# The second shift of VectorE's exponents as a transfer that adds a constant in place

## The chip, the cores and the metric

The kernel runs on one core of one Trainium2 chip. The metric is the device time of one execution in microseconds, the median of several runs. Five queues of instructions run beside each other: TensorE (PE) with its weight loads (PEld), VectorE (DVE), ScalarE (ACT), GpSimd (POOL) and SyncE (SP), which only issues transfers here. Each takes its instructions in the order of the program and waits on semaphores where it needs another's result.

## The reference

One transformer block with conditioning: six rows of modulation from `silu(c) @ w_mod`, then a layer norm, attention with 32 heads of 16 columns over 2,048 tokens, and a layer norm with a two-layer network of 1,376 columns.

```python
mod = (silu(c) @ w_mod).reshape(1, 6, 1, 512)       # sa, ca, ga, sb, cb, gb
h = layernorm(x) * (1 + ca) + sa
q, k, v = split(h @ wqkv)                            # 32 heads of 16
p = softmax(q @ k.T * 16 ** -0.5)                    # 2048 x 2048 for each head
x = x + ga * ((p @ v) @ wo)
h = layernorm(x) * (1 + cb) + sb
x = x + gb * (gelu(h @ w1 + b1) @ w2 + b2)
```

The attention asks for 32 x 2,048 x 2,048 exponentials, and that is most of the work.

## The kernel before

**Quads.** The attention goes through 32 quads: a block of 512 queries (four blocks) and four heads that sit on four groups of 32 partitions (eight such groups of heads). The last two quads are cut in halves of 256 queries, so that their end can begin earlier. For every quad there are 16 tiles of 128 keys and four heads, 64 tiles of 128 x 512 scores. Four heads' matmuls run side by side on PE, since each uses 32 rows or 32 columns of it.

**Two ways to an exponential.** A tile's scores are made by PE in a bank of PSUM (line 819) and then go one of two ways.

- ScalarE takes two or three banks at once and writes the exponential into `PB` as bfloat16 (line 1254). One matmul per tile then multiplies it with the values (line 1028).
- VectorE makes an approximation. The scores were scaled when `q` was made, so that 1,024 is one power of two. VectorE adds a bias and writes the sum as a 16-bit integer into `TB` (line 1349); read as a 16-bit float, these bits are roughly 2 to the score: exact at whole powers, straight between them. To flatten the error the kernel uses three such approximations, with the scores shifted by thirds of a power of two: the integers of the first (j = 0), the same plus `MJ[1]` (j = 1), the same plus `MJ[2]` (j = 2). Each has a matmul of its own, with the values scaled to match (`VE`, and `VV` for j = 1 and 2). So a tile on VectorE costs an evacuation, two shifts on VectorE (line 1383, for two tiles at once) and three matmuls with the values in place of one. Only six of the sixteen key tiles (`DKT`) have scaled values and may go this way.

Two tiles on VectorE make a unit. A unit's integers lie in a slot of `TB`; there are `NT` = 19 slots. A shift goes into the old slot if the matmuls that read it are done, and into a free slot otherwise. Before the change the second shift adds `MJ[2] - MJ[1]` to the result of the first.

**The order is planned when the program is built.** A planner walks through time with a clock for each engine and the cost of each instruction written in the code. At each moment the engine that is furthest behind takes its next step: `step_pe`, `step_act`, `step_dve`, or the GpSimd step. So the program's order on each engine comes out of these costs, and a small change moves everything behind it. `D_LOAD` is how much work VectorE may have ahead of it when PE makes scores for it (`dve_load` adds it up), `T_NEED` and `T_NEXT` how many slots must be free. Entries for the value matmuls are queued by head with the time at which they are expected (`put_entries`); PE takes them in that order. When PE has nothing that fits, the planner lets it issue a filler, a matmul with zeros (`pe_idle`, lines 1092 and 1095), so that its clock isn't lowered.

**GpSimd.** It scales the values, multiplies gates into weights, and multiplies each quad's output with the reciprocal of its sum (line 1328), which SP brings to it through DRAM as `rb`. The planner keeps VectorE's shifts and GpSimd's arithmetic apart in time: `plock` and `dlock` hold back the one while the other runs, and a dependency puts a GpSimd instruction beside one of VectorE's that reads PSUM.

The modulation, the projections, the layer norms and the network of the previous block (`sums`, `alone`) are fitted between by position. The last block's network stands alone at the end, from some 735 us on.

Of the kernel before, what the change touches and what calls it, by code (L numbers as in the profile page):

```python
# [10 lines left out]
ACT = mybir.ActivationFunctionType  # L11
ALU = mybir.AluOpType
# [3 lines left out]
I16 = mybir.dt.int16  # L16
F16 = mybir.dt.float16
# [3 lines left out]
P = 128  # L21
# [14 lines left out]
NV = 3  # L36
# [4 lines left out]
NPA = 5  # L41
NPB = 5
NP = 3 * NPA + 2 * NPB
NT = 19
KEEP = 0.72
NQM = 5
BIG = 8.0
# [2 lines left out]
D_BANKS = (6, 5)  # L50
BG_BANKS = (2, 5, 6)
BG_STRICT = False
D_LOAD = 2300.0
D_ALONE = 1400.0
A_SLACK = 1350.0
OVER = 180.0
# [7 lines left out]
LOCK_WAIT = 100.0  # L64
TIE = 60.0
T_NEED = 1
T_NEXT = 2
T_OPEN = 0.0
ROOT = 1000.0
ROOT_L = 700.0  # L70
# [17 lines left out]
def adaln_block(ctx: ExitStack, tc: tile.TileContext, A_x, A_wqkv, A_wo, B_x, B_w1, B_b1, B_w2, B_b2,  # L88
# [262 lines left out]
    pbp = att.enter_context(tc.tile_pool(name="pbp", bufs=1))  # L351
    PB = pbp.tile([P, NP, 512], BF16, name="PB")
    TB = pbp.tile([P, NT, 2, 512], I16, name="TB")
    RB = [odp.tile([P, 512], FP32, name=f"rb{par}") for par in range(2)]
    for par in range(2):
        nc.gpsimd.memset(RB[par], 0.0)
# [490 lines left out]
    def dve_load(t):  # L847
        w = max(0.0, clk["DVE"] - t)
        for s in evacs:
            w += 0.0 if s.only else s.dur  # L850
        for s in shifts:
            w += 331.0 * (NV - 1 - s["j"])
        w += 600.0 * sum(1 for x in d_fill)
        return w

# [53 lines left out]
    def pe_burst(t, z):  # L909
        bs = list(ZONES[z]) if z is not None else []  # L910
        x = EXTRA[z] if z is not None else None
        if x is not None and free[x] <= t and not (busy_sum[0] is None and reserve(t)):
            bs.append(x)
        take = []
        for r in lag_rows():
            if len(take) == len(bs):
                break
            if rowq[r] and item_ok(*rowq[r][0], t):
                take.append((r, 0))
        if z is not None and len(take) < len(bs):  # L920
            more = [(r, 1) for r, _ in take if len(rowq[r]) > 1 and item_ok(*rowq[r][1], t)]
            take += more[:len(bs) - len(take)]
        if z is not None and not take:
            return False
        picked = [(r, rowq[r][k]) for r, k in take]
        for r, x in picked:
            rowq[r].remove(x)
        used = [r for r, _ in take]
        dp = []
        if d_wanted(t):  # L930
            for r in d_rows(used):
                k = next_d(r, t)
# [12 lines left out]
                if u is None or len(u["it"]) + len(dp) == 2:  # L945
                    break
        if z is None and not dp:
            return False
        go("q")
        t0 = clk["PE"]  # L950
        rows = [r for r, _ in picked] + [r for _, r, _ in dp]
        first = len(set(rows))
        clk["PE"] = t0 + group(first) + (group(len(rows) - first) if len(rows) > first else 0.0)
        ready = clk["PE"] + L_PE
        qk([(b_, qi, kt, r) for (r, (qi, kt)), b_ in zip(picked, bs)] + [(b_, qi, kt, r) for b_, r, (qi, kt) in dp])
        for (r, (qi, kt)), b_ in zip(picked, bs):
            free[b_] = INF
        if z is not None:
            zone_busy[z] = True
            filled.append((z, [(qi, kt, r) for r, (qi, kt) in picked], clk["PE"] + L_PA))  # L960
        for b_, r, (qi, kt) in dp:
            free[b_] = INF
            if not units or len(units[-1]["it"]) == 2:
                s = next(i for i in range(NT) if tslot[i] <= t)
                tslot[s] = INF
                units.append({"it": [], "a": {"s": s}, "j": 0, "n": 0})
            u = units[-1]
            u["it"].append((qi, kt, r))
            todo[qi][r] += NV - 1
            claimed[qi][r] += 1  # L970
            d_fill.append((b_, u, len(u["it"]) - 1, ready))
            stat["d"] += 1
        stat["bursts"] += 1
        return True
# [363 lines left out]
    def step_dve(t):  # L1338
        if outs and outs[0][1] <= t:
            emit_out(outs.popleft()[0], t)  # L1340
            return True
        if d_fill and d_fill[0][3] <= t:
            b0, u, i, _ = d_fill[0]
            n = 1
            if (len(d_fill) > 1 and d_fill[1][1] is u and d_fill[1][3] <= t and d_fill[1][0] == b0 + 1):
                n = 2
            for _ in range(n):
                d_fill.popleft()
            made = nc.vector.tensor_scalar(out=TB[:, u["a"]["s"], i:i + n, :], in0=PS[:, b0:b0 + n, :], scalar1=T_BIAS,  # L1349
                                    scalar2=0.0, op0=ALU.add, op1=ALU.max)  # L1350
# [12 lines left out]
        if (units and units[-1]["n"] == 1 and len(units[-1]["it"]) == 1  # L1363
                and (sum(len(q) for q in rowq) < 10 or not any(left[units[-1]["it"][0][0]])
                     or t > units[-1]["at"] + 3000.0)):
            u = units[-1]
            u["it"].append(None)
            u["n"] = 2
            u["ok"] = t
            shifts.append(u)  # L1370
            put_entries(u, t)
        if take_evac("DVE", t):
            return True
        if run_alone("DVE", t):
            return True
        now = [] if plock[0] > t + LOCK_WAIT else [
            u for u in shifts if u["ok"] <= t and (u["a"].get("cons", INF) <= t or any(y <= t for y in tslot))]
        if now:
            u = max(now, key=lambda u: u["j"])
            a, j = u["a"], u["j"] + 1  # L1380
            n = sum(1 for it in u["it"] if it)
            s = a["s"] if a.get("cons", INF) <= t else next(i for i in range(NT) if tslot[i] <= t)
            made = nc.vector.tensor_scalar(out=TB[:, s, 0:n, :], in0=TB[:, a["s"], 0:n, :],  # L1383
                                           scalar1=float(MJ[j] - MJ[j - 1]), scalar2=None, op0=ALU.add)
            clk["DVE"] = max(t, plock[0] - 50.0) + 65.0 + 133.0 * n
            dve_log.append((clk["DVE"], made))
            dlock[0] = clk["DVE"]
            a["moved"] = clk["DVE"]
            if s != a["s"]:
                tslot[s] = INF  # L1390
                if "cons" in a:
                    tslot[a["s"]] = max(a["cons"], a["moved"])
            u["a"], u["j"], u["ok"] = {"s": s}, j, clk["DVE"] + 125.0
            if j == NV - 1:
                u["a"]["moved"] = 0.0
                shifts.remove(u)
                units.remove(u)
            put_entries(u, clk["DVE"] + L_DVE)
            return True
        return False  # L1400

    def put_entries(u, v):
        a, j = u["a"], u["j"]
        s = a["s"]
        cnt = [sum(1 for it in u["it"] if it)]

        def rel(done):
            cnt[0] -= 1
            if cnt[0] == 0:
                a["cons"] = done + L_FREE_D  # L1410
                if "moved" in a:
                    tslot[s] = max(a["cons"], a["moved"])

        for i, it in enumerate(u["it"]):
            if it is not None:
                qi, kt, r = it
                entries[qi][r].append((v, TB[:, s, i, :].bitcast(F16), kt, j, rel))

    def general_path():
        W_1, W_2, b1c = late["W_1"], late["W_2"], late["b1c"]  # L1420
# [88 lines left out]

    ENG = {"PE": step_pe, "ACT": step_act, "DVE": step_dve, "POOL": lambda t: run_alone("POOL", t)}
    rank = {"DVE": 0, "ACT": 1, "PE": 2, "POOL": 3}
    idle = dict.fromkeys(ENG, 0.0)
    tick = 20.0
# [55 lines left out]
```

## Time and profile before

| | |
|---|---|
| median of 3 runs | 764.57 us (764.04 to 765.09) |
| the profiled execution | 765.63 us |
| its span, first to last instruction | 763.9 us |
| mean granted TensorE clock | 0.992 |
| tiles through ScalarE | 377 pairs and 246 triples, 1,492 |
| tiles through VectorE | 556, and as many shifts of two |
| fillers on PE | 523 |
| GpSimd busy | 108.9 us of 763.9 |
| transfers issued by GpSimd | none |

A line of the groups names the program's line, the engine, the operation, what is written and read, their shapes and the count; behind the first bar stand the busy time of the group and the mean length of one instruction, behind the second the idle time of the engine just ahead of them and what ended it. An instruction's length includes its tail, in which the next one has begun already, so a mean times a count can exceed the busy time. A line of the stretches has the length, the busy time of PE, PEld, DVE, ACT and POOL with the number of instructions, the granted clock of PE, the share of time in which the transfer engines were busy, and GB/s.

### The profile page before, as it was taken

To read this page: it belongs to the slowest core of one execution; us is meant where nothing else is said; L and a number is where in the kernel's file an instruction comes from. 1 tells how busy PE (TensorE), PEld (TensorE's weight loads), DVE (VectorE), ACT (ScalarE), POOL (GpSimd) and SP (SyncE) were. 2 spreads that over 40 slices of the span, in tenths; PEclk is the share of its full clock that TensorE was granted. 3 is DMA by queue.
4 is the path that set the end of the run, shared out by engine and by line. 5 is a ranking of instruction groups with operands and counts; after the bars stand their busy time and mean duration, and the time that the engine had idled before them with its cause. 6 is when DMAs were issued, how large, how long until landed. Compare 5 with 4: busy or idle time off the path is not lost.

```text
span 763.9 us, 20459 instructions
## 1 busy us (share of the span) xinstructions
PE 737.2 (97%) x8478; PEld 258.7 (34%) x8478; DVE 700.5 (92%) x1450; ACT 721.7 (94%) x671; POOL 108.9 (14%) x134
## 2 busy tenths in 40 slices
PE   3999999999999999999999999999999999999997
PEld 2433233233333333332333333332333332333454
DVE  6859999699999999988999999999899999999982
ACT  2889999899999999999999999999999999999982
POOL 3460010214232010100001110100101110100110
PEclk9999999799999999999999999999999999999999
DMA  8300000041010000000010000000000000000000
GB/s 274 112 2 11 10 6 6 9 151 16 10 37 9 10 4 8 9 16 24 15 38 3 15 4 10 9 17 12 22 18 30 9 10 9 9 10 23 21 28 31
DMA packets 27572, 20.43 MB, mean 27 GB/s; under 512 B 13801, under 2 KB 23386, under 8 KB 27474
## 3 DMA queue, kind: packets, MB, share of 16 engines
q1 hardware_dynamic: 26946, 19.07, 9.0%
q8 instruction: 68, 1.11, 0.6%
q14 instruction: 30, 0.25, 0.1%
q10 hardware_dynamic: 528, 0.00, 0.0%
HBM read 16.45 MB, written 2.61 MB: 25 GB/s over the span
## 4 chain that ended last, share of the span: by engine, by line
PE 57%; ACT 26%; DVE 9%; issue 5%; DMA 2%; SPq 1%; POOL 0%; ACTq 0%; DVEq 0%
ACT PB L1254 23%; PE PS L819 20%; PE PS L1028 18%; PE PS L406 12%; DVE TB L1349 4%; DVE TB L1383 2%; ACT uG L614 2%; PE PS L1092 2%; DMA xb<-in_A_x_dram 1%; PE PS L720 1%; PE PS L708 1%; PE PS L1095 1%; PE PS L213 1%; DVE st L189 1%; ACT L1254 0%
## 5 line engine op out<-in xcount | busy, mean ns | idle before, releaser
L1254 ACT ACTIVATE PB<-PS 128x1024 bf16<-128x1024 f32 x623 | 679.3, 1299 | 9.5 <-PE PS L819 7.7
L1349 DVE TENSOR_SCALAR TB<-PS 128x512 int16<-128x512 f32 x556 | 368.3, 682 | 22.1 <-PE PS L819 20.6
L819 PE MATMUL PS<-qm,kT 32*128 32x512 bf16 (+1 forms) x2176 | 301.9, 372 | 5.8 <-ACT PB L1254 2.8
L1028 PE MATMUL PS<-PB,VE 128*32 128x512 bf16 (+1 forms) x1589 | 252.0, 374 | 0.3 <-ACT PB L1254 0.3
L1383 DVE TENSOR_SCALAR TB<-TB 128x1024 int16<-128x1024 int16 x556 | 221.9, 421 | 5.3 <-PE PS L1028 0.5
L1028 PE MATMUL PS<-TB,VV 128*32 128x512 f16 (+1 forms) x1174 | 219.8, 374 | 0.3 <-DVE TB L1383 0.2
L819 PEld LDWEIGHTS <-kT 32*128 32x128 bf16 x2176 | 81.1, 91 | 244.5 <-issue 236.0
L1028 PE MATMUL PS<-TB,VE 128*32 128x512 f16 (+1 forms) x587 | 148.4, 375 | 1.2 <-DVE o_sb L1304 1.2
L1028 PEld LDWEIGHTS <-VE 128*32 128x32 bf16 x2176 | 69.0, 94 | 82.2 <-issue 72.1
L1028 PEld LDWEIGHTS <-VV 128*32 128x32 bf16 x1174 | 55.0, 95 | 43.7 <-issue 38.7
L1092 PE MATMUL PS<-W_q,zero 128*32 128x256 bf16 x360 | 66.7, 273 | 1.8 <-DVE TB L1349 1.4
L1328 POOL TENSOR_TENSOR OT<-o_sb,rb 128x512 bf16<-128x512 f32 x15 | 19.1, 1274 | 252.4 <-DVE TB L1383 140.7
L1328 POOL TENSOR_TENSOR o_sb<-o_sb,rb 128x512 f32<-128x512 f32 x15 | 19.1, 1270 | 247.4 <-DVE TB L1383 199.2
L406 PE MATMUL PS<-W,uG 128*32 128x512 bf16 x528 | 44.8, 383 | 0.0
L406 PE MATMUL PS<-h2T,W 128*32 128x512 bf16 x528 | 43.4, 384 | 0.2 <-DVE TB L1349 0.2
L1092 PEld LDWEIGHTS <-zero 128*32 128x32 bf16 x360 | 33.0, 96 | 23.2 <-issue 8.4
L1095 PE MATMUL PS<-W_q,zero 128*32 128x256 bf16 x163 | 34.4, 276 | 0.0
L604 DVE TENSOR_SCALAR uG<-PS,b1c 128x512 bf16<-128x512 f32 x33 | 24.6, 744 | 0.2
L406 PE MATMUL PS<-W_o,OT 128*32 128x512 bf16 x272 | 21.0, 383 | 0.6 <-DVE OT L1289 0.6
L1304 DVE COPY o_sb<-PS 128x512 f32<-128x512 f32 x30 | 20.4, 680 | 0.0
L1331 POOL TENSOR_TENSOR OT<-OT,o_sb 128x512 bf16<-128x512 bf16 x15 | 17.4, 1162 | 20.8 <-DVE TB L1383 11.7
L406 PE MATMUL PS<-hT,W_q 128*32 128x512 bf16 x240 | 20.0, 384 | 0.2 <-DVE TB L1349 0.2
(110 smaller groups left out, 401.6 us busy)
## 6 DMA issues: line engine op xcount, KB each, us to landing
rb<-d SPq DMA_DIRECT2D x120, 32.0 KB
W_m<-in_w_mod_dram SPq DMA_DIRECT2D x3, 1024.0 KB
xr<-in_A_x_dram SPq DMA_DIRECT2D x4, 512.0 KB
out_dram<-ob SPq DMA_DIRECT2D x16, 128.0 KB
xb<-in_A_x_dram SPq DMA_DIRECT2D x3, 512.0 KB
W<-in_B_w_dram SPq DMA_DIRECT2D x1, 1376.0 KB
W<-in_B_w_dram SPq DMA_DIRECT2D x1, 1280.0 KB
xb<-in_A_x_dram SPq DMA_DIRECT2D x4, 128.0 KB
```

What stands on the lines that cost most here:

```text
L406: nc.tensor.matmul(out=ps[cols, :], lhsT=lhsT[:, cols], rhs=rhs, start=start, stop=stop)
L604: return lambda ps, e: nc.vector.tensor_scalar(out=T["u"][:, fc, :], in0=ps, scalar1=late["b1c"][:, fc:fc + 1], scalar2=None, op0=ALU.add)
L819: nc.tensor.matmul(out=bk(bank)[:, seg(qi, i)], lhsT=kT[32 * r:32 * r + 32, ch, kt[i] * P:(kt[i] + 1) * P], rhs=qm[(b, ch)][32 * r:32 * r ...
L1028: nc.tensor.matmul(out=PS[32 * r:32 * r + 32, 7, tok_of(qi)], lhsT=wt, rhs=src[:, seg(qi, i)], start=not started[qi][r], stop=todo[qi][r] ...
L1092: nc.tensor.matmul(out=PS[0:32, b_, 0:256], lhsT=zero, rhs=W_q[:, 0, 0:256], start=True, stop=True)
L1095: nc.tensor.matmul(out=PS[32 * o_:32 * o_ + 32, 7, c_:c_ + 256], lhsT=zero, rhs=W_q[:, 0, 0:256], start=False, stop=False)
L1254: nc.scalar.activation(out=PB[:, at:at + n, :], in_=PS[:, b0:b0 + n, :], func=ACT.Exp, bias=-KEXP * math.log(2.0), scale=math.log(2.0) / STEP)
L1304: made = nc.vector.tensor_copy(out=o, in_=bk(7))
L1328: return nc.gpsimd.tensor_tensor(out=o if par else ot, in0=o, in1=rb, op=ALU.mult)
L1331: return nc.gpsimd.tensor_tensor(out=ot, in0=ot, in1=o, op=ALU.add)
L1349: made = nc.vector.tensor_scalar(out=TB[:, u["a"]["s"], i:i + n, :], in0=PS[:, b0:b0 + n, :], scalar1=T_BIAS, scalar2=0.0, op0=ALU.add, op ...
L1383: made = nc.vector.tensor_scalar(out=TB[:, s, 0:n, :], in0=TB[:, a["s"], 0:n, :], scalar1=float(MJ[j] - MJ[j - 1]), scalar2=None, op0=ALU.add)
```

## The change

Both shifts can start from the first integers, as j = 2 is j = 0 plus `MJ[2]`. After the change the planner remembers the slot of j = 0 (`u["a0"]`) when the first shift goes into another slot. When the value matmuls of j = 0 have read it and the first shift has too, GpSimd issues a transfer that adds a constant array `step2`, filled with `MJ[2]`, to that slot in place: the transfer engines read the constant and the integers, add, and write. VectorE still makes every first shift. It also makes the second one where the first was made in place (there is no j = 0 left), and where the unit belongs to a quad whose end is near: `by_dve` says so when the running quad has fewer than `DMA_MIN` = 32 value matmuls left to issue for the unit's quad. On VectorE a second shift starts from j = 1 as before, or from j = 0 if that slot is free of readers.

The planner counts `DMA_ISSUE` = 1,000 ns of GpSimd for an issue and expects the result `L_DMA` = 4,500 ns later. Nothing holds VectorE's shifts back while GpSimd issues. Three other numbers of the planner change with it: one slot fewer (18, the constant needs the room), `D_LOAD` 1,800 for 2,300, and `T_NEXT` 1 for 2.

```diff
-NT = 19
+NT = 18
-D_LOAD = 2300.0
+D_LOAD = 1800.0
+DMA_MIN = 32
+DMA_ISSUE = 1000.0
+L_DMA = 4500.0
-T_NEXT = 2
+T_NEXT = 1
...
+    step2 = const.tile([P, 1, 512], I16, name="step2")
+    nc.gpsimd.memset(step2, MJ[2])
...
         for s in shifts:
-            w += 331.0 * (NV - 1 - s["j"])
+            w += 331.0 if s["j"] == 0 or by_dve(s, t) else 0.0
...
         now = [] if plock[0] > t + LOCK_WAIT else [
-            u for u in shifts if u["ok"] <= t and (u["a"].get("cons", INF) <= t or any(y <= t for y in tslot))]
+            u for u in shifts if u["ok"] <= t and (u["j"] == 0 or by_dve(u, t))
+            and (u["a"].get("cons", INF) <= t or u["j"] and u["a0"].get("cons", INF) <= t or any(y <= t for y in tslot))]
         if now:
             u = max(now, key=lambda u: u["j"])
             a, j = u["a"], u["j"] + 1
+            if j == 2 and u["a0"].get("cons", INF) <= t:
+                a = u["a0"]
...
-                                           scalar1=float(MJ[j] - MJ[j - 1]), scalar2=None, op0=ALU.add)
+                                           scalar1=float(MJ[j] - MJ[a["j"]]), scalar2=None, op0=ALU.add)
...
+    def by_dve(u, t):
+        q = min(it[0] for it in u["it"] if it)
+        return "s" not in u["a0"] or q < cur[0] or q == cur[0] and sum(todo[q]) < DMA_MIN
+
+    def step_pool(t):
+        for u in shifts:
+            a = u["a0"]
+            if u["j"] == 1 and a.get("cons", INF) <= t and a["read"] + 60.0 <= t and not by_dve(u, t):
+                n = sum(1 for it in u["it"] if it)
+                nc.gpsimd.dma_start(out=TB[:, a["s"], 0:n, :], in_=step2.to_broadcast([P, n, 512]), accum_op=ALU.add)
+                clk["POOL"] = t + DMA_ISSUE
+                shifts.remove(u)
+                units.remove(u)
+                u["a"]["moved"] = t
+                let_go(u["a"])
+                u["a"], u["j"] = {"s": a["s"], "j": 2, "moved": 0.0}, 2
+                put_entries(u, t + L_DMA)
+                stat["dma"] = stat.get("dma", 0) + 1
+                return True
+        return run_alone("POOL", t)
...
-    ENG = {"PE": step_pe, "ACT": step_act, "DVE": step_dve, "POOL": lambda t: run_alone("POOL", t)}
+    ENG = {"PE": step_pe, "ACT": step_act, "DVE": step_dve, "POOL": step_pool}
```

More of the change, by code (lines that the diff above doesn't have):

```diff
@@ L965, in pe_burst @@
                 tslot[s] = INF
-                units.append({"it": [], "a": {"s": s}, "j": 0, "n": 0})
+                units.append({"it": [], "a": {"s": s, "j": 0}, "a0": {}, "j": 0, "n": 0})
             u = units[-1]
@@ L1387, in step_dve @@
             dlock[0] = clk["DVE"]
[L1388 to L1395, printed above, removed]
+            tslot[s] = INF
+            new = {"s": s, "j": j}
+            if j == 1:
+                if s != a["s"]:
+                    a["read"] = clk["DVE"]
+                    u["a0"] = a
+            else:
+                for x in (u["a"], u["a0"]):
+                    x["moved"] = clk["DVE"]
+                    if x.get("s") not in (None, s):
+                        let_go(x)
                 shifts.remove(u)
                 units.remove(u)
+                new["moved"] = 0.0
+            u["a"], u["j"], u["ok"] = new, j, clk["DVE"] + 125.0
             put_entries(u, clk["DVE"] + L_DVE)
@@ L1400, in step_dve, with let_go @@
         return False
+    def by_dve(u, t):
+        q = min(it[0] for it in u["it"] if it)
+        return "s" not in u["a0"] or q < cur[0] or q == cur[0] and sum(todo[q]) < DMA_MIN
+    def let_go(x):
+        if "cons" in x and "moved" in x:
+            tslot[x["s"]] = max(x["cons"], x["moved"])
+    def step_pool(t):
[14 more added lines that the diff above has]
+        return run_alone("POOL", t)
     def put_entries(u, v):
         a, j = u["a"], u["j"]
-        s = a["s"]
         cnt = [sum(1 for it in u["it"] if it)]
@@ L1410, in rel @@
                 a["cons"] = done + L_FREE_D
-                if "moved" in a:
-                    tslot[s] = max(a["cons"], a["moved"])
+                let_go(a)
         for i, it in enumerate(u["it"]):
@@ L1416, in put_entries @@
                 qi, kt, r = it
-                entries[qi][r].append((v, TB[:, s, i, :].bitcast(F16), kt, j, rel))
+                entries[qi][r].append((v, TB[:, a["s"], i, :].bitcast(F16), kt, j, rel))
     def general_path():
```

## The prediction

> **What bounds the kernel now.** I read the page's shares by engine first, then a table of stretches, then the groups of instructions, then the waits, and last the rows that come nearest to the new transfers. Shares and chain first:
>
> ```profile
> PE 737.2 (97%) x8478; PEld 258.7 (34%) x8478; DVE 700.5 (92%) x1450; ACT 721.7 (94%) x671; POOL 108.9 (14%) x134
> ...
> PE 57%; ACT 26%; DVE 9%; issue 5%; DMA 2%; SPq 1%; POOL 0%; ACTq 0%; DVEq 0%
> ```
>
> Three engines are close to full and the chain changes hands between PE and ACT. The stretches (busy time of each engine, then the granted clock) show which of them has nothing left:
>
> ```profile
> 300.00:400.00 100.00, 98.90 (x1103) 32.05 (x1101) 92.58 (x187) 98.77 (x86) 7.40 (x6) 1.00 0.07 17
> 400.00:500.00 100.00, 98.88 (x1089) 31.79 (x1085) 96.75 (x200) 99.97 (x89) 11.09 (x10) 1.00 0.05 11
> 500.00:600.00 100.00, 98.87 (x1115) 32.99 (x1116) 95.43 (x201) 99.97 (x92) 7.77 (x7) 1.00 0.08 20
> 600.00:700.00 100.00, 99.81 (x1151) 33.88 (x1144) 96.70 (x201) 99.94 (x91) 9.73 (x9) 1.00 0.05 10
> ```
>
> The fourth number is ACT: 98.8 to 100 us of each 100. The third is DVE at 93 to 97. PE is as full, but part of it is filler, as the groups show (busy us, mean ns | idle before them and what ended it):
>
> ```profile
> L1254 ACT ACTIVATE PB<-PS 128x1024 bf16<-128x1024 f32 x377 | 399.1, 1133 | 1.7 <-PE PS L819 1.2 <-PE PS L1028 0.2
> L1254 ACT ACTIVATE PB<-PS 128x1536 bf16<-128x1536 f32 x246 | 382.1, 1553 | 7.8 <-PE PS L819 6.5 <-PE PS L1028 1.2
> L1349 DVE TENSOR_SCALAR TB<-PS 128x512 int16<-128x512 f32 x556 | 368.3, 682 | 22.1 <-PE PS L819 20.6
> L1383 DVE TENSOR_SCALAR TB<-TB 128x1024 int16<-128x1024 int16 x556 | 221.9, 421 | 5.3 <-PE PS L1028 0.5
> L1092 PE MATMUL PS<-W_q,zero 128*32 128x256 bf16 x360 | 66.7, 273 | 1.8 <-DVE TB L1349 1.4
> L1095 PE MATMUL PS<-W_q,zero 128*32 128x256 bf16 x163 | 34.4, 276 | 0.0
> ```
>
> So 523 matmuls (360 + 163) only keep PE occupied. ACT waited 9.5 us in all for scores. The bound between 40 and 735 us is ACT, with PE and DVE close behind: a tile of scores taken from ACT is time saved as long as DVE and PE can carry it.
>
> **What the change does to each engine**, counted from the order of the two built programs. Only 192 of 291 second shifts become transfers (one of them of a single tile); the others stay on DVE, which now makes 390 shifts for 556. DVE scores 579 tiles for 556; ACT 1,469 for 1,492, but in 422 pairs, 208 triples and one single for 377 and 246. PE has 394 fillers for 523, and 44 more attention matmuls behind the scores.
>
> *ACT.* Consecutive exponentials overlap, so the means are no price. The page has 679.3 us for all 623, and the two means are 0.420 us apart: 377a + 246(a + 0.420) = 679.3 gives a = 0.925 us for a pair, 1.345 for a triple. After: 422 x 0.925 + 208 x 1.345 + 0.5 = 670.6. ACT does 8.7 us less, all of it on the path.
>
> *DVE.* In the timeline two shifts in a row take 0.75 us and one 0.42, so 0.33 each; two evacuations 1.28 and one 0.68, so 0.60 each. -166 x 0.33 + 23 x 0.60 = -55 + 14 = -41 us. That alone saves nothing: DVE is not last. It is what pays for the 23 tiles, and the cover for the collisions below.
>
> *PE.* Four small matmuls run side by side in 0.22 us (the chain shows x4 in 0.22); 44 more are 11 such groups, +2.4 us. A filler of half the columns takes half of that, 0.11: 129 fewer are -14.2 us. PE has 11.8 us less to issue, which agrees with a span shorter by about 9. If PE were the true bound, 2.4 us would be the loss.
>
> *GpSimd.* 192 issues, queued among its 45 multiply-adds for the outputs and the weight gates. No row shows an issue on GpSimd. SP's take 0.32 to 1.92 us (first row below), GpSimd's smallest arithmetic 1.07 (the 4-wide power). I take 1.1 (the nearest on the engine itself): 211 us on an engine that is 14% busy, off the path. An issue queued right behind such arithmetic (34 times in the changed order) waits up to 1.27 us more, and that arithmetic in turn waits for its rows of rb and for the DVE instruction that it is put beside; these waits are within the time that the readers leave, below. The added 512-wide constant costs one fill at the start, 0.5 us as its neighbours (0.524), beside loads.
>
> *The transfer itself.* It is on the path only if it lands after its reader's turn on PE. In order of time: release of the old slot by PE, issue on GpSimd, data, completion. The rows nearest to it are SP's:
>
> ```profile
> L1324 SPq DMA_DIRECT2D rb<-d x120: 317/412/1922, 71.4 to 705.2; - x120
> ```
>
> ```profile
> SPq L1324 <- DMA d<-rp: 40.3, 30, 3.0
> SPq L1310 <- DMA d<-o_sb: 34.5, 30, 1.2
> ```
>
> The second fence is SP waiting for an 8 KB transfer to land behind its issue: 1.15 to 1.34 us on average, at worst 3.0. Data: 256 KB are written; in this stretch of 15 us the engines moved 147 GB/s at a share of 0.46 (the last two numbers), so 320 GB/s when full:
>
> ```profile
> 155.00:170.00 15.00, 15.00 (x170) 5.00 (x162) 14.28 (x30) 15.00 (x16) 3.04 (x5) 1.00 0.46 147
> ```
>
> That is 0.8 us, and 1.6 if reading the destination costs as much again: 192 of them fill 0.4 of the span. SP's small transfers for the reciprocals share these engines; GpSimd once waited 16.7 us for rb, and a quad's 22 us leave them room. Low end 0.2 (semaphore, guessed) + 0.3 + 1.15 + 0.8 = 2.5 us; high end 0.2 + 1.9 + 3.0 + 1.6 + 0.8 (a shift at its worst, below) = 7.5; I take 0.2 + 1.1 + 1.3 + 1.6 = 4.2. The Trainium skill (DMA: Bandwidth & Descriptors, Anatomy of one DMA) gives 2.0 us plus bytes over 436 GB/s for a transfer issued by GpSimd, an estimate of 2.6 us here without the second read; no run so far shows it, and by it none is late and the 1 us that I add below falls away.
>
> *When the reader comes.* In the changed program the matmul that waits for a transfer stands 41 to 125 matmuls behind the one that releases its slot; a tenth stand within 57, a quarter within 66, the middle at 78. PE issued 11 per us (x1103, x1089, x1115 per 100 us above), so 3.7 us at the shortest, 5.2, 6.0 and 7.1. At 4.2 us one in twenty or fewer is late, by under 0.5 us: 10 x 0.25, +2 us at most, of which ACT's queue of scores hides some. I take +1.
>
> *Collisions of DVE and GpSimd.* The kernel kept its shifts away from GpSimd's arithmetic, and nothing keeps them from the issues. What a meeting costs, two rows tell from both ends (ns at the least, the middle, the most):
>
> ```profile
> L1383 DVE TENSOR_SCALAR TB<-TB x556: 355/417/831, 58.9 to 733.5; 128x1024 int16<-128x1024 int16 x186
> ```
>
> ```profile
> L208 DVE TENSOR_SCALAR xb<-xb,mv,rs x16: 395/410/1117, 8.7 to 30.9; 128x512 bf16<-128x512 bf16 x16
> L208 DVE TENSOR_SCALAR uG<-xr,mv,rs x12: 401/404/1423, 246.2 to 604.4; 128x512 bf16<-128x512 bf16 x12
> ```
>
> A shift was held for 0.41 us at worst, a normalisation for 0.71 and 1.02. With 211 us of issues in the 690 us of attention (0.31), 120 of 390 shifts meet one: 0 to 120 us on DVE, against the 41 it gave up. I take 0.1 us each, 12 us, as the shift itself is the nearest row and its mean of 421 is hardly over its median: nothing on the path. The Trainium skill (SBUF — State Buffer, Who interferes with whom) states a port pair that the two share under an exclusive lock, the loser standing still for the whole instruction. The worst rows agree with it, as far as they go, since 1.02 us is near to a whole GpSimd instruction; by that rule every meeting costs up to the whole issue, which is the hard form of the second rival.
>
> Sum against the profiled execution (765.63 us; its span 763.9 and 1.7 around it): -8.7 + 1 = about -8, so 757.6. The median of the runs is 1.06 lower, 764.57: **756.5 us**. Not counted is the half clock of this execution, in which ACT is idle 2 us; it may come again or not:
>
> ```profile
> 137.00:142.00 5.00, 4.99 (x50) 1.59 (x46) 3.08 (x8) 4.68 (x5) 1.27 (x1) 0.55 0.01 3
> 142.00:148.00 6.00, 6.00 (x52) 1.24 (x48) 1.52 (x3) 4.27 (x4) 1.16 (x1) 0.52 0.00 0
> ```
>
> **Rivals.**
> 1. *The transfers land late.* Readers are taken in order on PE, so a late one holds all matmuls behind it. At a landing 6.0 us after the release the readers nearer than 66 matmuls wait, 57 us over all transfers; about two are in flight at a time and share a stall, so 28, and PE has 394 x 0.11 = 43 us of fillers to lose: the gain is about gone. That is the point from which it decides. At 6.5 us (72 matmuls) the waits add up to 100 us, shared 50, half of it lost in place of fillers: 757 + 25 = **782 us**. At the high end, 7.5, it would be over 800. For it: two steps have no row of their own. Against it: the middle estimate has 1.8 us to spare.
> 2. *DVE becomes the bound*, held up by GpSimd's issues. At 0.34 us for each of 120 meetings DVE gives back its 41 us: late evacuations hold PE's score banks and the 23 tiles are no longer paid for: **765 us**, no change. In the hard form, 1.02 us each, DVE has 122 - 41 = 81 us more than before; between 200 and 700 us it had some 20 idle, so 60 would show: **over 800**. Against it: those two rows are single worst cases.
> 3. *PE is the true bound* and the lighter ACT mostly waits: the score pairs cost more switches on PE. Only part of the 8.7 is had: **762 us**. For it: 57% of the chain is PE; against it: the fillers.
>
> **How the numbers follow.** A change under 0.2% (1.5 us) is about what a measurement of this kernel can't tell from none. Forecast (751 to 760): 0.50. Rival 3 (760 to 763): 0.12, still faster. Rival 2 without loss (763 to 766): 0.06. Rival 1 and the hard form of rival 2: 0.32, two thirds of it below 786. Faster 0.62, same 0.06, slower 0.32. The range goes from 749 (the 8.7, the half clock's 2, and a few us of ACT's waits gone) to 786, leaving out a tenth above and a little below; the forecast's own range is 751 to 760.
>
> **What will show it.** Exponentials near 670 us in all, ACT still at 99 of 100 us between 200 and 700, and DVE near 92 - 41/7.6, some 87%: the count is right. Waits of PE on a DMA into TB above 10 us in total show rival 1; shifts with a median well over 417 ns, and PE waiting for evacuations, rival 2; GpSimd busy or waiting over half of the span, a dearer issue than 1.1. The forecast is wrong if a transfer takes over 6 us from release to landing, or if each issue stops DVE for its whole length.

## The result and the profile after

The changed kernel takes 794.67 us (median of 4 runs, 792.44 to 797.18) against 764.31 us of the kernel before beside it: a ratio of 1.0397 (95% interval 1.0365 to 1.043), 30 us slower. The prediction was 756.5 us, 8 us faster; the range ended at 786. The profiled execution took 794.42 us, its span 792.7.

The page's shares by engine and its row for the queue of GpSimd's transfers (packets, MB, the share of 16 engines' span), after:

```profile
PE 743.7 (94%) x8393; PEld 248.8 (31%) x8393; DVE 683.6 (86%) x1309; ACT 718.7 (91%) x677; POOL 344.1 (43%) x327
...
q0 software_dynamic: 52096, 50.21, 44.1%
```

The share of every compute engine but GpSimd fell. No engine became the new bound; they wait for each other more. The stretches of after, as before (the fourth number is ACT's busy time, the one before the last the share of the transfer engines):

```profile
300.00:400.00 100.00, 97.83 (x1076) 30.02 (x1073) 87.51 (x161) 97.52 (x85) 40.86 (x34) 0.98 0.55 86
400.00:500.00 100.00, 93.31 (x988) 27.31 (x984) 85.76 (x164) 91.33 (x85) 43.21 (x37) 0.95 0.56 85
500.00:600.00 100.00, 96.40 (x1040) 28.18 (x1039) 90.38 (x168) 94.99 (x91) 50.44 (x41) 1.00 0.70 106
600.00:700.00 100.00, 95.79 (x1036) 30.50 (x1036) 92.44 (x181) 96.24 (x87) 41.16 (x35) 1.00 0.49 77
```

ACT had 98.8 to 100 us of each 100 before and has 91 to 97.5 now. The groups say what it waits for (busy us, mean ns | idle time before them and what ended it):

```profile
L1259 ACT ACTIVATE PB<-PS 128x1536 bf16<-128x1536 f32 (+2 forms) x631 | 677.3, 1212 | 38.5 <-PE PS L824 32.1
L1354 DVE TENSOR_SCALAR TB<-PS 128x512 int16<-128x512 f32 x579 | 383.5, 682 | 59.7 <-PE PS L824 56.8
L1428 POOL DMA_DIRECT2D TB<-step x192 | 235.9, 1541 | 276.5 <-PE PS L1033 201.4
...
L1033 PE MATMUL PS<-TB,VV 128*32 128x512 f16 (+1 forms) x1218 | 229.3, 377 | 20.6 <-DMA TB<-step 20.1
L1391 DVE TENSOR_SCALAR TB<-TB 128x1024 int16<-128x1024 int16 x390 | 173.4, 460 | 11.5 <-PE PS L1033 8.2
```

ACT was idle for 38.5 us ahead of its exponentials, 9.5 before: 29 us more, about the 28.8 us that the span has grown (792.7 - 763.9). It waited for scores, DVE waited for scores too (59.7 us for 22.1), and PE, which makes them, waited for transfers into `TB`. The view of the issuing line gives the length of an issue (least, middle, most, ns) and, in its last line, the time from an issue's start to the landing of its data:

```profile
L1428 POOL DMA_DIRECT2D TB<-step x192: 885/1228/4059, 62.0 to 758.3; - x192
...
DMA to landing us min/median/max: 3.6/4.8/10.7
```

The planner counted on 4.5 us for the latter, and 115 of the 192 transfers take longer. The waits of PE that the trace puts down to transfers, 20.1 us in 28 places, understate it. Taking every matmul that started within 0.4 us of the landing that it needs gives 63 of the 192 readers, and from the start of the matmul ahead of each to its own start 36.6 us passed in all, where matmuls otherwise start 0.09 us apart on average (11 per us): 36.6 - 63 x 0.09 = 31 us.

Three things could have cost the 30 us: the new order, the issues on GpSimd, and the time of the data. The experiments take them apart. All edits are to the changed kernel; medians stand beside 764.0 to 764.5 us of the kernel before, but for the last one, where it is named. One execution of a later version that took 784.16 us, at a granted clock of 0.978, is left out of its median.

### The profile page after: what moved, and what is told of

Its sections match the earlier page's. It is cut to its first block, busy times and chain, and to the rows that moved or that the text cites. A ratio compares the mean times of both kernels' runs of the same rounds, so it can differ in the third digit from the quotient of the medians.

```text
span 792.7 us, 20619 instructions
## 1 busy us (share of the span) xinstructions
PE 743.7 (94%) x8393; PEld 248.8 (31%) x8393; DVE 683.6 (86%) x1309; ACT 718.7 (91%) x677; POOL 344.1 (43%) x327
## 3 DMA queue, kind: packets, MB, share of 16 engines
q0 software_dynamic: 52096, 50.21, 44.1%
## 5 line engine op out<-in xcount | busy, mean ns | idle before, releaser
L1259 ACT ACTIVATE PB<-PS 128x1536 bf16<-128x1536 f32 (+2 forms) x631 | 677.3, 1212 | 38.5 <-PE PS L824 32.1
L1354 DVE TENSOR_SCALAR TB<-PS 128x512 int16<-128x512 f32 x579 | 383.5, 682 | 59.7 <-PE PS L824 56.8
L1428 POOL DMA_DIRECT2D TB<-step x192 | 235.9, 1541 | 276.5 <-PE PS L1033 201.4
L824 PE MATMUL PS<-qm,kT 32*128 32x512 bf16 (+1 forms) x2176 | 312.0, 373 | 8.4 <-DVE TB L1354 2.8
L1033 PE MATMUL PS<-TB,VV 128*32 128x512 f16 (+1 forms) x1218 | 229.3, 377 | 20.6 <-DMA TB<-step 20.1
L1391 DVE TENSOR_SCALAR TB<-TB 128x1024 int16<-128x1024 int16 x390 | 173.4, 460 | 11.5 <-PE PS L1033 8.2
L1097 PE MATMUL PS<-W_q,zero 128*32 128x256 bf16 x264 | 53.0, 274 | 1.7 <-DVE TB L1354 0.8
L1333 POOL TENSOR_TENSOR o_sb<-o_sb,rb 128x512 f32<-128x512 f32 x15 | 20.0, 1336 | 30.0 <-DVE TB L1391 11.9
L1100 PE MATMUL PS<-W_q,zero 128*32 128x256 bf16 x130 | 30.7, 277 | 0.0
L1097 PEld LDWEIGHTS <-zero 128*32 128x32 bf16 x264 | 23.4, 96 | 19.6 <-issue 11.1
L411 PE MATMUL PS<-W_o,OT 128*32 128x512 bf16 x272 | 25.3, 416 | 0.8 <-DVE TB L1354 0.7
L302 POOL TENSOR_SCALAR VV<-VE 128x512 bf16<-128x512 bf16 x12 | 17.9, 1492 | 13.3 <-DVE VE L297 12.7
```

The lines of the kernel that those rows point to most:

```text
L302: return nc.gpsimd.tensor_scalar(out=dst, in0=src, scalar1=WJ[j], scalar2=None, op0=ALU.mult)
L411: nc.tensor.matmul(out=ps[cols, :], lhsT=lhsT[:, cols], rhs=rhs, start=start, stop=stop)
L824: nc.tensor.matmul(out=bk(bank)[:, seg(qi, i)], lhsT=kT[32 * r:32 * r + 32, ch, kt[i] * P:(kt[i] + 1) * P], rhs=qm[(b, ch)][32 * r:32 * r ...
L1033: nc.tensor.matmul(out=PS[32 * r:32 * r + 32, 7, tok_of(qi)], lhsT=wt, rhs=src[:, seg(qi, i)], start=not started[qi][r], stop=todo[qi][r] ...
L1097: nc.tensor.matmul(out=PS[0:32, b_, 0:256], lhsT=zero, rhs=W_q[:, 0, 0:256], start=True, stop=True)
L1100: nc.tensor.matmul(out=PS[32 * o_:32 * o_ + 32, 7, c_:c_ + 256], lhsT=zero, rhs=W_q[:, 0, 0:256], start=False, stop=False)
```

## The experiments

**The order alone.** The issuing line is taken out and everything else stays in its place.

```diff
-                nc.gpsimd.dma_start(out=TB[:, a["s"], 0:n, :], in_=step2.to_broadcast([P, n, 512]), accum_op=ALU.add)
```

> The changed program with the 192 transfers left out and everything else in the same order (the third approximation of these units then reads unshifted integers, so that part of the result is not computed). Theory A, transfers that land late hold PE: about 757 us, the sum of the prediction without its late transfers, and PE's idle time back from 49 to about 27 us. Theory B, GpSimd's issues stop VectorE: also about 757, as no issue is left, with the shifts back from a mean of 463 ns to 421. Theory C, the new order itself is worse (more pairs, PE the true bound): it stays at 785 to 795.

759.09 us, ratio 0.9938 (0.9917 to 0.9959). The groups of this run:

```profile
L1259 ACT ACTIVATE PB<-PS 128x1536 bf16<-128x1536 f32 (+2 forms) x631 | 669.4, 1275 | 10.4 <-PE PS L824 7.7
L1354 DVE TENSOR_SCALAR TB<-PS 128x512 int16<-128x512 f32 x579 | 383.0, 682 | 48.4 <-PE PS L824 45.7
...
L1391 DVE TENSOR_SCALAR TB<-TB 128x1024 int16<-128x1024 int16 x390 | 159.1, 424 | 5.7 <-PE PS L1033 2.5
```

The exponentials take 669.4 us (670.6 was forecast) and ACT's idle time ahead of them is nearly as before (10.4 us for 9.5). So the order is not at fault: without its transfers it gains 5.1 us. That is all that the transfers had to win.

**The issues without their data.** The same 256 pieces per transfer, but each of 32 columns (64 bytes) in place of 512.

```diff
-                nc.gpsimd.dma_start(out=TB[:, a["s"], 0:n, :], in_=step2.to_broadcast([P, n, 512]), accum_op=ALU.add)
+                nc.gpsimd.dma_start(out=TB[:, a["s"], 0:n, 0:32], in_=step2[:, :, 0:32].to_broadcast([P, n, 32]), accum_op=ALU.add)
```

> The changed program, each transfer adding to the first 32 columns of each tile alone: as many issues, descriptors and waits, a sixteenth of the bytes (fifteen sixteenths of the second shift are left out). A: the landing after the issue falls from 4.8 us to about 3.3, few readers wait, 758 to 765 us. B: the issues are the same, so the shifts keep a mean of some 460 ns and the time stays above 785. C: 785 to 795.

766.9 us, ratio 1.004 (1.0025 to 1.0054). The view of the issuing line:

```profile
L1428 POOL DMA_DIRECT2D TB<-step x192: 885/1254/3993, 61.9 to 732.3; - x192
...
DMA to landing us min/median/max: 2.6/3.0/6.0
```

and two of its groups:

```profile
L1259 ACT ACTIVATE PB<-PS 128x1536 bf16<-128x1536 f32 (+2 forms) x631 | 673.2, 1233 | 17.2 <-PE PS L824 12.0
...
L1391 DVE TENSOR_SCALAR TB<-TB 128x1024 int16<-128x1024 int16 x390 | 172.7, 459 | 6.4 <-PE PS L1033 3.3
```

The issues are as long as in the full version, the data is there 1.8 us sooner, the trace has no wait of PE for a transfer, and 27.8 us of the loss are gone. So the greater part is the time of the data. The other 7.8 us (766.9 - 759.09) come with the issues: the shifts' busy time is 172.7 us for 159.1, and ACT's idle time 17.2 for 10.4. The timeline shows where the shifts lose it: the 155 that overlap an issue take 492 ns on average, the 197 that overlap neither an issue nor GpSimd's arithmetic 414, and 155 x 0.078 = 12 us. PE's waits for VectorE's evacuations (line 1354) rise from 2.1 us in the order alone to 6.0 here, and ACT's waits for scores from 7.7 to 12.0.

**A plain copy.** The addition is left out, so the transfer writes the same bytes without reading the old ones. **Half the pieces.** Only the first 32 columns of a unit's first tile, 128 pieces for 256.

```diff
-                nc.gpsimd.dma_start(out=TB[:, a["s"], 0:n, :], in_=step2.to_broadcast([P, n, 512]), accum_op=ALU.add)
+                nc.gpsimd.dma_start(out=TB[:, a["s"], 0:n, :], in_=step2.to_broadcast([P, n, 512]))      # copy
+                nc.gpsimd.dma_start(out=TB[:, a["s"], 0, 0:32], in_=step2[:, 0, 0:32], accum_op=ALU.add) # half
```

> The changed program, the transfers copying the constant over the slot without the addition (the third approximation reads a constant, so that part of the result is not computed): the same issues and bytes written, no read of the destination. A: packets of 1 KB go back from 111 ns to about 46, the data part from 1.8 us to 0.75, the landing from 4.8 to about 3.8, and the time to 765 to 775. B and C: above 785.

> The changed order, each transfer adding to the first 32 columns of its first tile alone (nearly all of the second shift is left out): half the descriptors of the sliver, the same number of issues. If what the sliver still loses (766.9 us against 759.1 without transfers) goes by the length of an issue on GpSimd: issues near 0.9 us, shifts with a mean near 440 ns, 761 to 764 us. If it goes by the number of issues alone: 766 to 768. If it comes from the planner's order: as the sliver too.

The copy takes 760.32 us (0.9955; 0.9936 to 0.9974), half the pieces 758.47 us (0.9928; 0.9909 to 0.9947), the order alone 759.09. Both are faster than any theory had them (765 to 775 and 761 to 764). The issuing line, the queue and the shifts in the copy:

```profile
L1428 POOL DMA_DIRECT2D TB<-step x192: 573/724/1552, 62.0 to 724.1; - x192
...
DMA to landing us min/median/max: 2.0/2.8/5.0
```

```profile
q0 software_dynamic: 15328, 50.21, 19.3%
...
L1391 DVE TENSOR_SCALAR TB<-TB 128x1024 int16<-128x1024 int16 x390 | 163.4, 435 | 6.4 <-PE PS L1033 3.3
```

and the issuing line and the shifts with half the pieces:

```profile
L1428 POOL DMA_DIRECT2D TB<-step x192: 850/905/2946, 62.2 to 723.0; - x192
```

```profile
L1391 DVE TENSOR_SCALAR TB<-TB 128x1024 int16<-128x1024 int16 x390 | 160.6, 428 | 5.6 <-PE PS L1033 2.3
```

The mean issue is 1.54 us with 256 pieces and an addition, 1.06 with 128, 0.74 in the copy; the price of all issues is 7.8, -0.6 and 1.2 us. With them go DVE's shifts, 13.6, 1.5 and 4.3 us over the 159.1 of the order alone. So an issue is not dear as such, but a long one of many pieces is; whether by its length or by its pieces these runs don't tell, as both fall together. And the same 50.21 MB land in 2.8 us when nothing is added: what makes the data slow is the addition, together with the smaller packets in which it goes (52,096 for 15,328). It takes the engines 0.441 x 792.7 / 192 = 1.82 us for each transfer, the copy 0.193 x 759 / 192 = 0.76.

**The other numbers alone.** All second shifts are left to DVE; the slot fewer, `D_LOAD` and `T_NEXT` stay.

```diff
-        return "s" not in u["a0"] or q < cur[0] or q == cur[0] and sum(todo[q]) < DMA_MIN
+        return True
```

> The planner's three other numbers alone: all second shifts stay on VectorE, with 18 slots, a load of 1,800 and one more free slot. ScalarE gets 393 pairs and 231 triples, 674 us by 0.925 and 1.345 for 679. A and B: 760 to 766, no loss without transfers. C, the numbers themselves cost time: above 770.

770.18 us, ratio 1.0091 (1.0056 to 1.0126): without transfers these numbers cost 6 us. The 11.1 us between this run and the first experiment (770.18 - 759.09) come from taking 180 shifts off DVE (390 for 570), with the changes in the order that follow from it.

**Room for the data in the plan.** The planner expects the result after 7 us and counts 1.6 us for an issue; then the same order with the transfers left out.

```diff
-DMA_ISSUE = 1000.0
-L_DMA = 4500.0
+DMA_ISSUE = 1600.0
+L_DMA = 7000.0
```

> The changed kernel with the planner told what was measured: a landing 7.0 us after the issue (4.5 before) and 1.6 us of GpSimd for an issue (1.0 before); nothing is left out. Theory A, 28 us of the loss are readers placed too early: PE's waits on transfers fall from 20 us to under 5 and the time to 764 to 772, the 8 us of the issues remaining. Theory B, the issues stop VectorE whatever the readers do: above 780, since there are 204 issues for 192.

> The kernel planned with a landing of 7.0 us, its transfers left out (204 second shifts are not computed), order unchanged. If the loss of that kernel (800.7 us) lies in the order itself, because value matmuls are queued in turn and a reader that stands later holds those behind it and the slots of ScalarE's results: 780 to 795. If it lies in what the transfers do on the chip: 757 to 765.

800.67 us with the transfers (1.049; 1.0456 to 1.0523), 793.59 without them (1.0388; 1.0323 to 1.0452). ACT's waits for the value matmuls (us in total, times, longest), with them and without:

```profile
ACT PB L1259 <- PE PS L1033: 27.4, 22, 3.3
```

```profile
ACT PB L1259 <- PE PS L1033: 26.2, 22, 3.3
```

The late data is cured: 2 of 204 readers start within 0.4 us of their landing, with 2.3 us lost ahead of them. But now the order itself is 34.5 us worse than that of the first experiment (793.59 - 759.09). ACT waits for line 1033, the value matmuls, because its output has no free slot in `PB`: PE takes the entries of a head in turn, so entries that wait longer for a transfer hold back the exponentials queued behind them. That is 26.2 of the 46.3 us that ACT is idle ahead of the exponentials when the transfers are left out. Another 11.3 us, for scores, lie between 176 and 206 us and have another cause: VectorE waited 6.1 us for the sums that SP brings through DRAM (`dall`), PE 6.2 us for VectorE, and PE's granted clock was 0.50 from 184.8 to 205.3 us. The issues seem to cost 7.1 us here (800.67 - 793.59), about the 7.8 of before, but the executions without transfers spread over 9 us (790.75 to 799.85). So in this planner the lateness wasn't planned away at no cost: the order either stalls PE or fills `PB`. Neither theory of the first forecast (764 to 772; above 780 by the issues) had this.

**Longer pieces.** The constant is made twice as wide, so that each partition's share is one piece of 2 KB: 128 pieces for 256, the whole computation.

```diff
-    step2 = const.tile([P, 1, 512], I16, name="step2")
+    step2 = const.tile([P, 1024], I16, name="step2")
...
-                nc.gpsimd.dma_start(out=TB[:, a["s"], 0:n, :], in_=step2.to_broadcast([P, n, 512]), accum_op=ALU.add)
+                nc.gpsimd.dma_start(out=TB[:, a["s"], 0:n, :].rearrange("p a n -> p (a n)"), in_=step2[:, 0:n * 512], accum_op=ALU.add)
```

> The changed kernel with the constant as 1,024 columns, so that a transfer reads and writes one run of 2 KB on each partition in place of two of 1 KB; the order stays. If the length of an issue (1.54 us) and part of the landing go by the number of descriptors: issue near 1.0 us, landing near 4.2 for 4.8, and 775 to 785 us. If the addition costs by bytes alone: as the change, 790 to 797.

777.94 us, ratio 1.0192 (1.0154 to 1.023), 16.7 us better than the change as made.

```profile
L1428 POOL DMA_DIRECT2D TB<-step x192: 850/886/2637, 61.8 to 740.0; - x192
...
DMA to landing us min/median/max: 3.0/4.3/9.4
```

```profile
q0 software_dynamic: 27648, 50.21, 38.3%
```

The mean issue is 1.02 us, the engines' time per transfer 1.54, the readers near their landing 45 for 63 and the time ahead of them 17.8 us for 36.6. Both terms fell.

What makes landings uneven shows when the transfers are sorted by how many earlier ones were still on their way at the end of their own issue (medians from there to the landing, in us; number of transfers; five transfers with four ahead are left out):

| on their way | 0 | 1 | 2 | 3 |
|---|---|---|---|---|
| the change | 2.68 (50) | 3.16 (79) | 4.20 (52) | 5.58 (10) |
| longer pieces | 2.62 (55) | 3.10 (71) | 3.88 (48) | 5.00 (15) |
| plain copy | 1.85 (80) | 2.06 (78) | 2.37 (29) | 2.53 (4) |
| 64-byte pieces | 1.45 (92) | 1.43 (93) | 1.42 (7) | - |

Issues follow each other after as little as 0.73 us and each keeps the engines for 1.82: they queue. Transfers of 64-byte pieces, whose data needs 0.57 us, don't.

**A planner that counts the queue.** With longer pieces, the planner keeps a clock for the transfer engines, lets GpSimd issue only while little is queued, and expects the result 1.5 us after the queue's end. Three settings, with at most 1.6, 0.8 and 1.6 us queued ahead of an issue, `D_LOAD` 2,300, 1,800 and 2,000, and `DMA_MIN` 32, 40 and 48, leave 185, 150 and 138 transfers. The third also lets the planner expect the reciprocals later (`rb` and `dall`).

```diff
-        for u in shifts:
+        for u in shifts if dma_free[0] <= t + Q_DMA else ():
...
-                put_entries(u, t + L_DMA)
+                dma_free[0] = max(t + DMA_ISSUE, dma_free[0]) + T_DMA
+                put_entries(u, dma_free[0] + L_DMA)
```

> Runs of 2 KB, and a planner that counts the transfer engines as a queue: an issue of 1.05 us, 1.55 us of the engines for each transfer, one behind the other, a landing 1.5 us after that; no issue while more than 1.6 us of work is queued; a load of 2,300. 185 transfers, nothing left out. If readers wait because transfers queue behind each other: PE's waits on transfers under 4 us and 757 to 766 us. If issue and addition cost time apart from that: 772 to 782, as the wide runs alone (777.9).

> As the kernel with the queue, with no issue while more than 0.8 us is queued, no transfers in the last 40 value matmuls of a quad, a load of 1,800: 150 transfers. Queueing: 758 to 766 us. Issue and addition: 770 to 778, less than with 185 by their number.

> The kernel with the queue, 138 transfers, and a planner that gives the reciprocals' transfers on SP's queue more time (8.0 us and 9.0 us for 6.0 and 6.5), so that GpSimd's multiplications wait less for them and the issues behind them come on time; no issue above 1.6 us of queue, none in the last 48 value matmuls of a quad. If the long single waits of the two kernels with the queue (up to 7 us) came from GpSimd waiting for rb: no wait of PE on a transfer above 2 us, 759 to 766 us. If not: 772 to 778 again.

775.36 us (1.0139; 1.0103 to 1.0175), 775.26 (1.0139; 1.0117 to 1.0162) and 775.87 (1.0163; 1.0145 to 1.018): hardly better than longer pieces alone. The forecasts by the queue alone (757 to 766 and 758 to 766) fell, and so did that for the third, no wait above 2 us and 759 to 766. What is left are a few long waits. Three of them in the second setting (us in total, times, longest):

```profile
POOL OT L1335 <- DMA rb<-d: 36.7, 6, 9.9
...
POOL b1c L547 <- DMA b_bf<-in_B_b_dram: 12.0, 1, 12.0
...
PE PS L1035 <- DMA TB<-step: 10.9, 3, 7.2
```

GpSimd stood before its own arithmetic for `rb`, and that was taken for the cause. The third setting cut these waits (9.4 us, once), but PE's waits for transfers stayed at 11.9 us, with one of 10. The timeline of the second setting could have told: PE's longest wait, 7.2 us, is for a transfer that GpSimd issued after 12.0 us before `b1c`, not before `rb`, and the next, 3.3 us, for one that landed 7.5 us after its issue, while the next block's weights were loaded. The third setting's timeline (start, length, engine, line, what, idle time before it) shows the place:

```profile
183.43 0.19 POOL L549 CAST b1c<-b_bf 128x11 f32<-128x11 bf16 x1 [11.56 <-DMA b_bf<-in_B_b_dram]
...
185.28 1.80 POOL L1434 DMA_DIRECT2D TB<-step  x2
...
188.65 0.59 PE L1037 MATMUL PS<-TB,VV 128*32 128x512 f16 x1 [10.02 <-DMA TB<-step]
```

GpSimd waited 11.6 us to convert the next block's biases, whose load SP had issued behind 2.7 MB of weights; two issues stood behind it.

**The biases loaded first.** SP issues the loads of the biases ahead of the weights'; all else as in the third setting.

```diff
-        nc.sync.dma_start(out=W_1[:, :, 0:F], in_=B_w1.rearrange("(j p) n -> p j n", p=P))
...
         nc.gpsimd.tensor_scalar(out=W_2[lr:lr + 1, NFC - 1, :], in0=W_2[lr:lr + 1, NFC - 1, :], scalar1=1.0 / BIG,
                                 scalar2=None, op0=ALU.mult)
+        nc.sync.dma_start(out=W_1[:, :, 0:F], in_=B_w1.rearrange("(j p) n -> p j n", p=P))
```

(The two loads into `W_2` move with it.)

> The version before this one (138 transfers in long runs, the planner counting the transfer engines as a queue, 775.87 us) kept one single wait of PE on a transfer, 10.0 us, and ScalarE lost 10.1 us to it. Just ahead of that transfer's issue GpSimd stood 11.6 us before its conversion of the next block's biases, whose load SP had issued behind 2.7 MB of weights. Here SP issues the loads of the biases ahead of those of the weights; nothing else is changed, and the whole computation is there. Theory 'GpSimd's own queue': the wait of GpSimd for the biases falls to 3 to 6 us, PE's longest wait on a transfer to under 4 us, and the time falls by 5 to 10 us, to 766 to 771. Rival 'the transfers themselves': the long wait of PE stays above 7 us, since the data was late behind the weights' 2.7 MB on the transfer engines, and the time stays at 774 to 778. Below 764 neither expects.

772.8 us beside 762.13 of the kernel before, ratio 1.0143 (1.0124 to 1.0162): against 1.0163 (1.0145 to 1.018) the intervals overlap.

```profile
175.09 0.19 POOL L545 CAST b1c<-b_bf 128x11 f32<-128x11 bf16 x1 [3.42 <-DMA b_bf<-in_B_b_dram]
...
176.94 1.95 POOL L1434 DMA_DIRECT2D TB<-step  x2
...
185.36 0.58 PE L1037 MATMUL PS<-TB,VV 128*32 128x512 f16 x1 [6.94 <-DMA TB<-step]
```

Each theory had half of it: GpSimd's wait fell to 3.4 us, PE's only to 6.9, and the time lies between their ranges (766 to 771 and 774 to 778). The issues come 8.3 us sooner, but these two transfers land 7.5 and 8.0 us after the end of their issue, where one alone takes 2.5 in this run. Their first packet started 4.5 us after the first issue began; for a transfer alone it is 1.5. The stretches of this run show what else was on the engines:

```profile
174.00:178.00 4.00, 4.00 (x49) 1.19 (x52) 3.81 (x7) 4.00 (x4) 2.75 (x4) 1.00 0.84 261
178.00:182.00 4.00, 0.43 (x6) 0.00 (x0) 1.14 (x4) 1.58 (x2) 0.89 (x1) 1.00 0.99 299
182.00:186.00 4.00, 0.64 (x6) 0.20 (x6) 0.00 (x0) 0.00 (x0) 0.00 (x0) 0.67 1.08 245
186.00:190.00 4.00, 4.00 (x27) 0.80 (x27) 2.32 (x4) 1.98 (x2) 0.00 (x0) 0.50 0.24 63
```

The engines were full (0.84 to 1.08): the weights, issued later than before, cross them ahead of the two transfers and beside them. PE stood until 185.4 us, and ACT and DVE had nothing more from 180 on. The wait of PE is 6.9 us for 10.0, as much shorter (3.1) as the profiled execution (770.59 for 773.81).

The wait costs more than its length. While PE stood, its granted clock fell to 0.50, at 183.4 us, and stayed there until 200.4; ACT was busy for only 9.6 of the 15 us from 185.4 to 200.4. From 178 to 200.4 us ACT was idle for 11.2 us in all, and that is about as much as its idle time ahead of the exponentials, 20.4 us, exceeds the 9.5 of before. In the third setting it is the same: clock 0.50 from 180.6 to 204.5, ACT idle for 14.3 us from 178 on, 23.4 us in all.

No version with the whole computation beats the kernel before; the last of them is 1.4% slower, with 138 transfers. What its own order would take without transfers was not measured, so how much of its loss is order and how much transfers stays open.

## Why the prediction was wrong

By the medians the 30.5 us (794.67 - 764.19) are: the order -5.1, the issues +7.8, the data's landing +27.8. The prediction's sum had -8.7, 0 and +1.

- **The transfer itself, 4.2 us: right for one, and the step that failed is that it was priced as one.** A transfer with nothing ahead takes 0.50 us from release to issue (mean of all), 1.2 for the issue and 2.7 to land: 4.4 us. But 142 of 192 had one to four others ahead, and the mean issue is 1.54 us. (1.1 was taken for it as GpSimd's smallest arithmetic, but line 199 of the kernel before, 4 wide too, took 0.29.) From release to landing they took 5.2 us in the middle, 6.5 at the upper quarter, 7.5 at the upper tenth and 11.7 at most; a third took over the 6 us that were named as the sign of being wrong. The working had both halves of the queue, 192 transfers filling 0.4 of the span and "about two in flight at a time", and used the second only to share stalls, not to lengthen landings.
- **"One in twenty late, +2 at most".** The readers came where forecast (6.7 us after the release in the middle; 7.1 forecast), but one fixed landing was held against a spread of readers. With a spread on both sides, 63 of 192 found their data not there, or only just. These stalls reached ACT: from the 64-byte version to this one its idle time rises by 21.3 us (38.5 - 17.2) and the exponentials' busy time by 4.1 (677.3 - 673.2), together 25.4, and the profiled executions are 25.7 us apart (794.42 - 768.75).
- **Rival 1 had the mechanism and not the size**: 782 us, reached at a common landing of 6.5 us; its point of decision, 6.0, lies between the middle and the upper quarter of the measured landings. It counted half of a stall as lost in place of fillers. But the fillers stand at fixed places in the program's order, and a PE that has waited for data issues them all the same: 264 + 130 in the profile, the 394 of the plan.
- **Collisions: 12 us on DVE, right; "nothing on the path", wrong.** The 64-byte version's shifts were busy 13.6 us longer, and the kernel lost 7.8: this term, put at nothing, is the second that failed. The cover, 41 us that DVE gave up, is a sum over the kernel: a long shift at the wrong moment can hold up an evacuation, then PE's scores, then ACT. The waits of the 64-byte version fit that path; no run shows it for a single shift. The hard form of rival 2, each meeting at the full length of an issue, is out: 155 shifts met an issue, and the meeting made them 0.08 us longer on average.
- **ACT: -8.7 us in work (9.9 measured in the first experiment), -5.1 in time.** In that profile the exponentials ended 8.9 us sooner than before (725.2 for 734.1 us), and what follows them took 2.0 us longer (31.8 for 29.8). That leaves 6.9; the medians are 5.1 apart.
- **The estimate by the Trainium skill** (DMA: Bandwidth & Descriptors, Anatomy of one DMA), 2.6 us for 256 KB, agrees with the plain copy (2.0/2.8/5.0) and not with the addition (3.6/4.8/10.7). The same section calls the building of descriptors small; here the mean issue goes from 1.06 to 1.54 us as 128 pieces become 256, and the kernel from 758.47 to 766.9.

Of the signs named ahead, three came: waits of PE on transfers above 10 us (rival 1), DVE at 86% (87% forecast), and GpSimd busy or waiting before an issue for 236 + 277 of 793 us, with an issue dearer than 1.1. The last shows little, as GpSimd waits for releases anyway; the issue's mean is the better sign. Exponentials came to 677.3 us, not 670: fewer of them overlap when ACT idles, as their mean says, 1,212 ns for 1,275 in the order alone.

## What to carry to other kernels

A transfer that takes work from an engine is to be priced as a queue: the time that each keeps the transfer engines, against the shortest distance between two issues, and whatever else crosses those engines; then the spread of landings stands against the spread of readers. Giving the late ones more room is not free where readers are taken in order, since it fills the buffers behind them. One long wait can cost as much as many short ones, as PE's granted clock may be halved behind it. And a transfer issued by a compute engine stands behind that engine's own waits, and a long issue disturbs its neighbour: as few and as long pieces as the shape allows.

## What the runs showed of the hardware

- A transfer that adds in place keeps the engines twice as long as a copy, and more in short pieces. The copy went in packets of 4 KB at 189 ns (middle value), 47 for each KB; the addition in packets of a piece each, 188 ns for 2 KB (94 for each KB) and 112 for 1 KB. For 256 KB that is 0.76, 1.54 and 1.82 us of all 16 engines.
- The same bytes went in 52,096 packets with the addition and in 15,328 without it, and the issue on GpSimd took 1,228 ns with it (middle value), 724 without, and 886 with the addition and half as many pieces.
- A shift that met a GpSimd issue was rarely held for all of it. In the changed kernel 154 of 390 overlapped one and took 485 ns on average, at most 1,072; the 198 that overlapped neither an issue nor GpSimd's arithmetic took 416, at most 430. The longest, 1,509 ns, lay beside a multiplication of GpSimd; without any issue, in the order alone, one beside such a multiplication took 1,380.
- Beside 2.7 MB of weights on another queue, two transfers of 256 KB landed 7.5 and 8.0 us after the end of their issue, for 2.5 us alone.
- While PE stood for 6.9 and 10.0 us its granted clock fell from 1.00 to 0.50, and it stayed there for 17.1 and 23.9 us.
